# Eight array places for the state matmuls of a chunked scan, with pairs of PSUM banks and other opening fillers

## The chip, the core and the metric

The kernel runs on one core of a Trainium2 chip. A core has a matmul engine (TensorE: PE for the matmuls, PEld for the loads of their weights in the traces), a vector engine (VectorE, DVE), a scalar engine (ScalarE, ACT), a general engine (GpSimd, POOL) and a queue engine (SyncE, SP) that here issues nearly all DMAs. Each works through its own instructions in order; semaphores order them against each other. The metric is the device time of one execution in microseconds (us). Data lie in an on-chip memory of 128 partitions (SBUF); matmuls write to eight accumulation banks (PSUM) of 128 partitions by 512 float32 values each, which VectorE and ScalarE read.

## What is computed

A chunked linear-attention scan over 4 batches of 8 heads, 768 positions, head size 32 and state size 16, followed by a feed-forward network on the 3072 tokens of 256 features. The weights of the network arrive as float64 and are split on the chip into a high and a low part.

```python
for c in range(nc):                       # chunks of the sequence
    cum = np.cumsum(la, axis=-1)          # la: log of the decays of the chunk
    L = np.exp(cum[:, :, :, None] - cum[:, :, None, :]) * causal
    M = np.einsum('bhin,bhjn->bhij', Cc, Bc) * L
    y[:, :, sl] = einsum('bhij,bhjd->bhid', M, xc) + einsum('bhin,bhnd->bhid', Cc, state) * exp(cum)
    state = decay_full * state + sum_j(B_j x_j decay_from_j)
...
h = (x @ w1) * (x @ w2) @ w3              # x: the scan's y, heads side by side
return h @ w_out
```

## The kernel before

**Tiling.** The kernel uses chunks of 48 positions, so there are 16 chunks, and two of them make a slice: 8 slices of 96 positions of 4 batches, 384 tokens. Heads go in pairs: one head of a pair lies on partitions 0 to 63, the other on 64 to 127 (16 rows of carried state and 48 of x each), so that 16 pairs cover the 32 heads. w3 and w_out are first multiplied into one matrix (steps `v.M`), and then each slice needs only `up` (x by w1 and w2, 8 tiles of features, two halves, tasks `l{slice}.{tile}.0` and `.1`, six float32r matmuls of 384 columns each), a gate (`.a` a copy on ACT, `.g` a multiply on DVE, `.h` and `.l` the split into high and low parts) and `down` (tasks `z{slice}.{0..2}`, with `y...` for the way out).

**A chunk's steps** (function `chunk`, from L371). `D0`, `D1`: the differences of the cumulative logs by matmul, 384 columns into one bank each. `E0`, `E1`: their exponential on ACT into R. `B0`, `B1`: POOL scales B's columns in R. `C`: the products of B and C, 16 float32 matmuls on 32-row by 64-column places of the array (eight places), into four banks. `M0` to `M3` (`weigh`, L400): DVE multiplies R by one of these banks each, 128 by 192. `Y` (L424): py, 32 float32 matmuls, each with one head's 64 rows as weights' rows, 32 columns and 64 moving columns, so on a 64-row by 32-column place. Its output is the next state (16 columns) and y transposed (48 columns). The column quarter q of four goes with row half q % 2, so four of the eight such places are used, and all output goes to one bank. `Z` (L437): DVE transposes the state part of py; `x0` to `x3` (`carry`, L440): four copies of it into XE for the next chunk, on the engine that the plan names. `h`, `l` (L449, L450): ACT and DVE split y out of py into the high and low parts that `up` takes.

**Banks.** `at_of` (L222) gives the bank of step k of chunk c (0, 1: D; 2 to 5: C; 6: py). From chunk 7 on these are banks 0 to 3 and, for py, bank 7; before, they rotate through banks 0 to 3. Banks 4 to 6 are a ring of three on which `up` and `down` tiles take turns in the order of the text `ORDER` (L22, L187 to L196). Bank 7 holds the product of w3 and w_out until that is done.

**Order.** The order of all engines is written out by hand: `PLAN` (L29) names every task, and each engine runs its part in the order of the text. A suffix names the engine (`:a` ACT, `:v` DVE, `:p` POOL). `+12` stands for 12 matmuls of bfloat16 zeros, 512 columns wide (`keep_clock`, L635): they compute nothing that is used.

**Weights.** `from_f64` (L458) makes the tasks of a piece of 128 by 512 float64 weights: `.D` its DMAs on SP into one of six staging slots (ST), `.A` and `.Y` mostly on ACT, `.L`, `.S` on DVE, `.H` the high part on the engine that the plan names and `.P` the low part on DVE. w0 to w7 are the pieces of w1 and w2, o0 to o3 those of w_out, v0 to v15 those of w3. `a.save` writes the cumulative logs to DRAM, and the tasks `c{n}.K`, from chunk 2 on, load them back chunk by chunk; `c{n}.X` loads x, `c{n}.T` B and C, `s{n}.N` B again in another layout. All are issued by SP in the order of the plan.

Of the kernel before, what the change touches and what calls it, by code (L numbers as in the profile page):

```python
# [7 lines left out]
F32 = mybir.dt.float32  # L8
# [6 lines left out]
ALU = mybir.AluOpType  # L15
# [19 lines left out]
w3.A:a l0.1.0 c1.Z w3.Y:a w2.L s1.N c1.x0:p c3.X w2.S c1.x1:p c2.D0 l0.1.1 c1.x2:p c2.E0 l0.0.g w2.H:p l0.1.a  # L35
w5.D w4.A:a w3.L c2.D1 c1.x3:p w2.P:v c2.E1 w4.Y:a +2 l0.2.1 w3.S w3.H:v c2.C c3.T w3.P:v c2.B1 w6.D c2.B0
l0.2.0 c2.M3 w7.D c2.M2 c2.M0 c2.M1 c3.D1 l0.2.a o1.D w4.L c3.D0 c3.E1 c2.Y w4.S c3.E0 c3.B1 l0.1.g c3.B0 o0.D
l0.3.1 w5.A:a c2.Z w4.H:p o2.D l0.2.g c2.h c2.x0:p l0.3.0 w4.P:v w5.Y:a c2.x3:p c4.T c2.x1:p c2.l c2.x2:p l0.4.0
l0.3.a w5.L w5.S c3.C l0.4.a c4.K l0.3.g w6.A:a w5.H:p l0.4.1 c3.M0 c3.M1 w6.Y:a c3.M3 c3.M2 l0.4.g c3.Y o3.D
w5.P:v w6.L l0.5.0 c3.Z w6.S c3.x0:p c3.h s2.N l0.5.1 c3.x2:p l0.5.a c3.l w6.H:p o1.A:a w7.A:v l1.0.1 c3.x3:p  # L40
o1.Y:a w6.P:v c3.x1:p v0.D l1.0.0 l0.5.g w7.Y:a o1.L o1.S l1.1.0 l1.0.a w7.L o0.A:a v3.D l1.1.1 w7.S o0.Y:a
l1.0.g w7.H:p o2.A:v v1.D l0.6.0 l1.1.a w7.P:v o2.Y:a c5.T l1.1.g l0.6.1 c4.X o0.L l0.6.a o0.S c5.K o1.H:a
# [58 lines left out]
def kernel(  # L101
# [88 lines left out]
    for op in ORDER.split():  # L190
        sl, ft = map(int, op.split(".")) if "." in op else (int(op), None)
        for k in [(sl, tk) for tk in range(NTT)] if ft is None else [(sl, ft, i) for i in range(2)]:
            pl_bank[k] = bank[4 + ring % 3]
            ring += 1
# [521 lines left out]
```

## Time and profile before

| | us |
|---|---|
| time, median of 3 runs | 281.46 (281.34 to 282.18) |
| the profiled execution's own time | 281.39 |
| its span, first to last instruction | 279.6 |

The page of the profile gives the busy time of each engine, the last chain of work and the costliest groups of instructions. In a group's row, `out<-in` are the program's tiles, then the form, the count, the busy time in us, the mean of one in ns, and the idle time of the engine before them with who ended it. Two things help in reading it: a float32 matmul leaves two records where a float32r one leaves one, and the end of a matmul is modelled and includes its way through the array, so that matmuls overlap; what one costs is read from the start of one to the start of the next. Three groups that belong to the steps of the change:

```profile
L158 PEld LDWEIGHTS bank<-rr,xe 64*32 64x32 f32 x1024 | 15.2, 107 | 5.5 <-issue 3.9
L394 ACT ACTIVATE rr<-bank 128x384 f32<-128x384 f32 x32 | 14.9, 492 | 9.8 <-PE bank L158 8.3
L167 POOL TENSOR_TENSOR rr<-bn,rr 128x128 f32<-128x128 f32 x32 | 15.9, 507 | 47.2 <-ACT rr L394 46.3
```

They are the weight loads of Y, the exponentials E and the scalings B.

### The profile page before, as it was taken

What the parts mean: (1) busy time and instruction counts of PE and PEld (TensorE: products, weight loads), DVE (VectorE), ACT (ScalarE), POOL (GpSimd) and SP (SyncE); (2) the same over time, 40 slices, a digit from 0 to 9 for tenths busy, and PEclk for the clock granted to TensorE, in tenths of its full rate; (3) what the DMA queues carried; (4) which work ended last, traced back from release to release, by engine and by line L of the source; (5) the groups of instructions that cost most, each with busy time, mean ns of one, the idle gap of its engine ahead of it and who ended that gap; (6) DMA issues with size and microseconds to landing.
All of it is one profiled execution on the core that took longest, in us unless ns stands there. A gap on an engine that the chain in (4) does not pass through costs nothing.

```text
span 279.6 us, 7296 instructions
## 1 busy us (share of the span) xinstructions
PE 273.8 (98%) x2957; PEld 242.6 (87%) x2957; DVE 155.5 (56%) x326; ACT 145.8 (52%) x280; POOL 105.6 (38%) x160
## 2 busy tenths in 40 slices
PE   8999999999999999999999999999999999999995
PEld 2466899998999998889998999999998998999884
DVE  5699999999999858354544153415251442122110
ACT  5496799999547377243561354335441543134211
POOL 8806550424423269581241236204520533044200
PEclk9999999999999999999999999999999999999999
DMA  5968988788831010225130320222011000100011
GB/s 164 289 189 255 351 281 267 221 293 283 267 115 39 4 52 0 70 77 160 33 80 21 78 69 16 89 71 82 11 30 45 15 2 0 43 15 0 21 49 46
DMA packets 22710, 29.31 MB, mean 105 GB/s; under 512 B 5524, under 2 KB 12948, under 8 KB 22676
## 3 DMA queue, kind: packets, MB, share of 16 engines
q1 hardware_dynamic: 22628, 28.81, 33.8%
q8 instruction: 23, 0.38, 0.6%
q14 instruction: 11, 0.09, 0.1%
q10 hardware_dynamic: 48, 0.03, 0.0%
HBM read 25.54 MB, written 3.29 MB: 103 GB/s over the span
## 4 chain that ended last, share of the span: by engine, by line
PE 90%; DMA 3%; SPq 2%; DVE 2%; issue 1%; POOL 0%; ACT 0%; DVEq 0%
PE bank L158 90%; SPq L161 2%; DMA cd<-gf 2%; DMA st<-in_w_dram 1%; DVE vl L167 1%; DVE gf L167 0%; DVE rr L167 0%; DVE wo L167 0%; POOL gf L167 0%; ACT rr L394 0%; POOL rr L167 0%; ACT ob L164 0%; DVE zz L437 0%; POOL gf L164 0%; DVE zero L268 0%
## 5 line engine op out<-in xcount | busy, mean ns | idle before, releaser
L158 PE MATMUL bank<-xt,w 128*128 128x384 f32 x768 | 146.2, 341 | 0.5
L158 PEld LDWEIGHTS bank<-xt,w 128*128 128x128 f32 x768 | 132.1, 188 | 5.9 <-DVE w L167 0.9
L167 POOL TENSOR_TENSOR g<-gf,g 128x384 fp32r<-128x384 f32 x52 | 55.6, 1081 | 62.1 <-ACT g L164 59.1
L158 PE MATMUL bank<-wo,g 128*128 128x256 f32 (+1 forms) x392 | 68.5, 334 | 0.0
L158 PEld LDWEIGHTS bank<-wo,g 128*128 128x128 f32 x392 | 59.5, 188 | 7.9
L167 DVE TENSOR_TENSOR gf<-gf,bank 128x384 f32<-128x384 f32 x64 | 35.2, 550 | 50.2 <-PE bank L158 45.0
L164 ACT CAST g<-gf 128x384 fp32r<-128x384 f32 x64 | 31.2, 514 | 36.5 <-DVE gf L167 36.4
L164 ACT COPY gf<-bank 128x384 f32<-128x384 f32 x64 | 31.5, 494 | 16.3 <-PE bank L158 16.2
L167 DVE TENSOR_TENSOR ob<-ob,bank 128x256 f32<-128x256 f32 x23 | 9.6, 419 | 45.4 <-ACT ob L164 45.4
L164 ACT COPY ob<-bank 128x256 f32<-128x256 f32 x24 | 9.0, 373 | 49.0 <-PE bank L158 46.6
L167 POOL TENSOR_TENSOR rr<-bn,rr 128x128 f32<-128x128 f32 x32 | 15.9, 507 | 47.2 <-ACT rr L394 46.3
L164 ACT COPY st<-st 128x512 uint16<-128x512 uint16 x23 | 31.6, 1398 | 1.1 <-DVE mag L482 0.7
L167 DVE TENSOR_TENSOR rr<-bank,rr 128x192 f32<-128x192 f32 x64 | 19.2, 348 | 5.6 <-POOL rr L167 2.7
L164 POOL COPY xe<-zz 16x256 f32<-16x256 f32 x28 | 14.6, 520 | 16.9 <-DVE zz L437 15.9
L497 DVE SCALAR_TENSOR_TENSOR mag<-mag,st 128x512 uint32<-128x512 uint32 x28 | 20.2, 723 | 0.7
L158 PEld LDWEIGHTS bank<-rr,xe 64*32 64x32 f32 x1024 | 15.2, 107 | 5.5 <-issue 3.9
L394 ACT ACTIVATE rr<-bank 128x384 f32<-128x384 f32 x32 | 14.9, 492 | 9.8 <-PE bank L158 8.3
L158 PE MATMUL bank<-wfh,vh 128*128 128x256 f32 x64 | 18.8, 293 | 0.0
L158 PE MATMUL bank<-rr,xe 64*32 64x64 f32 x1024 | 18.2, 218 | 0.4 <-issue 0.4
L158 PE MATMUL bank<-wfh,vl 128*128 128x256 f32 x64 | 17.9, 279 | 0.0
L158 PE MATMUL bank<-wfl,vh 128*128 128x256 f32 x64 | 17.9, 279 | 0.0
L479 ACT ACTIVATE mag<-st 128x512 f32<-128x512 f32 x22 | 15.3, 704 | 0.4 <-DMA st<-in_w_dram 0.3
(68 smaller groups left out, 210.4 us busy)
## 6 DMA issues: line engine op xcount, KB each, us to landing
st<-in_w3t_dram SPq DMA_DIRECT2D x16, 512.0 KB
st<-in_w_dram SPq DMA_DIRECT2D x16, 256.0 KB
xe<-in_x_dram SPq DMA_DIRECT2D x32, 96.0 KB
bc<-in_Bt_dram SPq DMA_DIRECT2D x8, 320.0 KB
bc<-in_Ct_dram SPq DMA_DIRECT2D x8, 320.0 KB
bn<-in_Bn_dram SPq DMA_DIRECT2D x8, 256.0 KB
st<-in_w_out_dram SPq DMA_DIRECT2D x4, 512.0 KB
out_dram<-ob SPq DMA_DIRECT2D x16, 96.0 KB
```

Of the source, the lines that this page charges most:

```text
L158: return tc.keep_in_program_order(nc.tensor.matmul(*args, **kw))
L161: return ins({None: nc.sync, "a": nc.scalar}[eng].dma_start(*args))
L164: return ins(nc.scalar.copy(*args) if eng == "a" else {"v": nc.vector, "p": nc.gpsimd}[eng].tensor_copy(*args))
L167: return ins({"v": nc.vector, "p": nc.gpsimd}[eng].tensor_tensor(*args))
L394: ins(nc.scalar.activation(R[:, hf * G8:(hf + 1) * G8, N:], v["pd", hf], AF.Exp))
L479: ins(nc.scalar.activation(v["mag"], v["wh"], AF.Copy, scale=2.0 ** -112))
L497: ins(nc.vector.scalar_tensor_tensor(mi, mi, 3, v["wh"].bitcast(U32), ALU.logical_shift_left, ALU.bitwise_or))
```

## The change

**Y on eight places.** The host swaps the two heads of each pair in odd batches, so that their rows lie in the other half. Y then goes through pairs of batches: for the even batch the column quarters 0, 1, 2, 3 with row halves 0, 1, 0, 1, and for the odd one the quarters 1, 0, 3, 2 with row halves 0, 1, 0, 1, eight places in a row. Even batches go to one bank and odd ones to another. Before chunk 7 these are banks 0 and 1; from chunk 7 on, bank 7 and one bank of the ring, for which `ORDER` has an entry (`c7` to `c15`). Each carry becomes two copies (on two engines where the plan names two). Before chunk 7, `Z`, `h` and `l` stay one instruction each, over the pair of banks; from chunk 7 on each becomes two, one for each bank, the ring's bank first.

**C and M in pairs of banks.** Banks 0 and 1, and 2 and 3, become one tile each of two banks. C always goes to these four; `M0` and `M1` multiply two banks at once. D of chunks 2 to 15 always uses banks 2 and 3.

**Order.** In slice 3 the plan takes the order of the later slices, with Y of one chunk directly ahead of C of the next. In slices 4 to 6, `Z`, `h` and `l` of a chunk come right behind Y and ahead of the next chunk's M.

**Opening.** The first fillers are 2 bfloat16 zero matmuls and 2 of float32 zeros (`*2`) in place of 12; `+7` before Y of chunk 1 becomes `*1 +3` and `+4` before the first `up` becomes `*1`. The float32 zeros lie in the last staging slot and are set by one more memset at the start. The fillers write bank 6 in place of 7. The DMAs of w2 (`w2.D`) are issued behind `a.save` in place of before it. The H step of w0 goes to POOL, `w1.Y` behind `c1.h`, and `k.R1` behind the carries of chunk 0.

The diff, cut to its core:

```diff
-+12 c0.C b.m01:v b.m10:v c0.D0 c1.X b.m11:v k.L1 w2.D c0.D1 a.scan c0.E0 k.R0 a.t0:p c1.D0 a.r0:p c0.E1 c0.B0
-w0.A:a c0.B1 c1.D1 c0.M0 c0.M1 a.t1:p c1.E0 c0.M2 a.r1:p c0.M3 w0.Y:v c1.E1 c0.Y c1.B0 a.save c1.B1 w0.L k.R1
-c1.C c2.X c0.Z c0.x0:v c0.x1:a w3.D c0.x3:a c0.x2:v c1.M0 c0.h c1.M1 w1.A:a c1.M2 c1.M3 w0.S w1.Y:a +7 c1.Y
-w0.H:v w0.P:v c1.h c2.K w2.A:a c0.l c1.l +4 l0.0.0 w2.Y:a w4.D w1.L w1.S l0.0.1 c2.T l0.0.a w1.H:v w1.P:v c3.K
++2 *2 c0.C b.m01:v b.m10:v c0.D0 c1.X b.m11:v k.L1 c0.D1 a.scan c0.E0 k.R0 a.t0:p c1.D0 a.r0:p c0.E1 c0.B0
+w0.A:a c0.B1 c1.D1 c0.M0 a.t1:p c1.E0 a.r1:p c0.M1 w0.Y:v c1.E1 c0.Y c1.B0 a.save c1.B1 w2.D w0.L c1.C c2.X c0.Z
+c0.x0:va c0.x1:ap c0.x2:vp c0.x3:ap k.R1 w3.D c0.h c1.M0 w1.A:a c1.M1 w0.S *1 +3 c1.Y w0.H:p c1.h w1.Y:a c2.K
+w2.A:a c0.l w0.P:v c1.l *1 l0.0.0 w2.Y:a w4.D w1.L w1.S l0.0.1 c2.T l0.0.a w1.H:v w1.P:v c3.K w3.A:a l0.1.0 c1.Z
...
-l4.0.h c11.B1 l4.1.1:4 l4.1.a l4.0.l:p l4.2.0:4 l4.1.g l4.1.h l4.2.1:4 l4.2.a l4.1.l:p c10.Y l4.2.g l4.2.h c11.C
-c10.Z s6.N l4.2.l:p l4.3.0:4 c10.h c11.M0 c11.M1 c10.x0:a c10.x1:v c10.x2:a l4.3.1:4 c10.x3:v l4.3.a c13.K c10.l
+l4.2.0:4 l4.1.g l4.1.h l4.2.1:4 l4.2.a l4.1.l:p c10.Y l4.2.g l4.2.h c10.Z c10.h c10.l c11.C s6.N l4.2.l:p
+l4.3.0:4 c11.M0 c10.x0:a c10.x1:v c10.x2:a l4.3.1:4 c10.x3:v l4.3.a c13.K l4.4.0:4 c11.M1 l4.3.g l4.3.h l4.4.1:4
...
+    PAIR = [ps.tile([P, 2, 512], F32, name=f"bank{i}") for i in range(2)]
+    bank = [PAIR[i // 2][:, i % 2] for i in range(4)] + [ps.tile([P, 512], F32, name=f"bank{i}") for i in range(4, 8)]
...
+    zerof = ST[:, NST - 1, 0:512]
...
         if c < CPS:
-            return bank[(0, 1, 2, 3, 4, 5, 6 if c == 0 else 1)[k]]
-        return bank[(7 * c + k) % 4 if c < CPS * (NLAG + 1) - 1 else (0, 1, 0, 1, 2, 3, 7)[k]]
+            return bank[((4, 5, 5, 7), (6, 4, 0, 1))[c][k]]
+        if k == 3 and c >= CPS * (NLAG + 1) - 1:
+            return pl_bank[False, (c,)]
+        return bank[(2, 3, 0 if c < CPS * (NLAG + 1) - 1 else 7, 1)[k]]
...
+        def weigh(hf):
+            t = R[:, hf * G8:(hf + 1) * G8, N:].rearrange("p (k g) s -> p k g s", k=2)
+            pc = PAIR[hf][:, :, :G8 // 2 * T].rearrange("p k (g s) -> p k g s", s=T)
+            tt("v", t, pc, t, ALU.mult)
...
+                for b2 in range(B2):
+                    for u, qs in enumerate(((0, 1, 2, 3), (1, 0, 3, 2))):
+                        po = py[0][:, u] if len(py) == 1 else py[1 - u][:, 0]
+                        for q in qs:
+                            h2 = (q + u) % 2
+                            g, rows = (2 * b2 + u) * HP + 2 * kt + q // 2, slice(64 * h2, 64 * h2 + 64)
+                            mm(po[32 * q:32 * q + 32, kt * B2 + b2], xe[rows, g], R[rows, g, :], start=True, stop=True)
...
+                for t, u in zip(py, us):
+                    ins(nc.vector.transpose(ZZ[:, u].rearrange("p u k b d -> p u (k b) d"), t[:, :, :, 0:32]))
...
+                for u, eu in zip((1, 0), e * 2):
+                    h2 = (q + u) % 2
+                    copy(eu, xn[64 * h2:64 * h2 + N, u, q // 2], ZZ[32 * q:32 * q + N, u].rearrange("p k b d -> p b k d"))
...
-    def keep_clock(n):
+    def keep_clock(n, z):
         for _ in range(n):
-            mm(bank[7], zero[:, 0:P], zero, start=True, stop=True)
+            mm(bank[6], z[:, 0:P], z, start=True, stop=True)
```

More of the change, by code (lines that the diff above doesn't have):

```diff
@@ L190 @@
     for op in ORDER.split():
-        sl, ft = map(int, op.split(".")) if "." in op else (int(op), None)
-        for k in [(sl, tk) for tk in range(NTT)] if ft is None else [(sl, ft, i) for i in range(2)]:
-            pl_bank[k] = bank[4 + ring % 3]
+        kind, k = op[0], tuple(map(int, op.strip("cz").split(".")))
+        for k in [k + (i,) for i in range(2)] if kind not in "cz" and len(k) == 2 else [k]:
+            pl_bank[kind == "z", k] = bank[4 + ring % 3]
             ring += 1
-        if ft is None:
-            DOWNS.append(sl)
+        if kind == "z" and k[0] not in DOWNS:
+            DOWNS.append(k[0])
     passing = ctx.enter_context(ExitStack())
```

166 lines of the change are left out of this document (87 added, 79 removed), and 3 rows, old and new, of the table ORDER.

## The prediction

> **What bounds the kernel now.** I read the page first: the busy times, the chain that ended last, the row of the small matmuls that the change touches.
>
> ```profile
> span 279.6 us, 7296 instructions
> PE 273.8 (98%) x2957; PEld 242.6 (87%) x2957; DVE 155.5 (56%) x326; ACT 145.8 (52%) x280; POOL 105.6 (38%) x160
> PE 90%; DMA 3%; SPq 2%; DVE 2%; issue 1%; POOL 0%; ACT 0%; DVEq 0%
> L158 PE MATMUL bank<-rr,xe 64*32 64x64 f32 x1024 | 18.2, 218 | 0.4 <-issue 0.4
> ```
>
> TensorE is busy 98% of the span, and 90% of the last chain is its own work. The fourth line is py, step Y: 1024 records for 16 chunks, 64 a chunk; each of its 32 float32 matmuls leaves two. An average over stages hides who else is full, so next the table by stage (length, then busy us of PE, PEld, DVE, ACT, POOL, each with its count; the second row counts only instructions that write or read the carried states), and the chain of waits in order of time near its end.
>
> ```profile
> 28.00:77.00 49.00, 48.82 (x570) 45.00 (x559) 47.82 (x94) 42.69 (x61) 19.10 (x33) 1.00 0.87 281
> 27.00:77.00 50.00, 4.68 (x256) 3.87 (x256) 0.00 (x0) 0.00 (x0) 8.91 (x16) 1.00 0.87 281
> 76.53 0.47 DVE gf L167
> ...
> 77.05 199.22 PE bank L158 x2034
> ```
>
> There are three stages. From 28 to 77 us, while the float64 weights are converted, **two** engines are full: DVE works 47.82 of 49.00 us, and the chain reaches PE at 77.05 by way of a DVE instruction. From 77.05 to the end PE works 199.22 us without a break, while DVE has 155.5 - 47.8 = 107.7 us of work for the other 230. Before 28 us lies an opening of fillers and waits. Y of four chunks, 2 to 5, falls between 27 and 77 us (x256), two lie before and ten behind. So a PE saving counts in full after 77 us, and before only as far as DVE can follow.
>
> **The main part: py on eight places.** PE's timeline in two late slices (start, length, group):
>
> ```profile
> 155.80 2.25 PE L158 MATMUL bank<-xt,w 128*128 128x384 f32 x12
> 157.89 0.50 PE L158 MATMUL bank<-rd,ld 102*128 102x384 bf16 x2
> ...
> 187.35 4.49 PE L158 MATMUL bank<-xt,w 128*128 128x384 f32 x24
> 191.77 1.10 PE L158 MATMUL bank<-rr,xe 64*32 64x64 f32 x64
> 192.79 0.59 PE L158 MATMUL bank<-bc 32*64 32x96 f32 x32
> 193.31 4.43 PE L158 MATMUL bank<-xt,w 128*128 128x384 f32 x24
> 197.58 0.50 PE L158 MATMUL bank<-rd,ld 102*128 102x384 bf16 x2
> ```
>
> From its start to the next start Y takes 192.79 - 191.77 = 1.02 us and C 0.52. Inside them, by short windows (PE busy with the matmuls that run in the window, old ones that still drain included; the first three rows count only Y, the last two only C):
>
> ```profile
> 191.76:191.84 0.08, 0.07 (x4) 0.07 (x8) 0.00 (x0) 0.00 (x0) 0.00 (x0) 1.00 0.00 0
> 191.84:191.90 0.06, 0.06 (x8) 0.06 (x12) 0.00 (x0) 0.00 (x0) 0.00 (x0) 1.00 0.00 0
> 191.90:191.96 0.06, 0.06 (x12) 0.06 (x11) 0.00 (x0) 0.00 (x0) 0.00 (x0) 1.00 0.00 0
> ...
> 192.79:192.92 0.13, 0.13 (x8) 0.13 (x16) 1.00 0.00 0
> 192.92:193.17 0.25, 0.25 (x32) 0.25 (x31) 1.00 0.00 0
> ```
>
> Y runs in rounds of four: the second and third window are cut at a round's length, 0.056 us, and each adds four to the four of the first. 16 rounds: 0.08 for the first, 14 x 0.056, 0.16 for the last until C starts, together 1.02. C, with its eight places, starts eight in its first 0.13 us and the other 24 in 0.25 (x32 with the first eight still draining): rounds of eight every 0.083 for 96 columns, 0.87 ns a column, the pace of Y (0.056 / 64 = 0.87). So eight places at once cost no more than four, in four banks and with a weight load before each matmul. Eight starts must fit into one round: four took under 0.03 (x4 in a 0.06 window), C's eight under 0.083; I take them to fit 0.056.
>
> Y after: eight rounds. First 0.08 to 0.13 (Y's own and C's), six times 0.056, the last 0.16 to 0.22 (192.79 + 0.52 less its last round's start at 192.79 + 0.13 + 2 x 0.083). That is 0.58 to 0.69; I take 0.64, **0.38 saved a chunk**, 6.1 over 16. Bounds: 0.44 at best; below, a loss (the slower rival).
>
> **Merged blocks.** In slice 3, C of 9, Y of 8, Y of 9 and C of 10 stood apart between up matmuls; now Y of 8 and C of 9, and Y of 9 and C of 10, are neighbours. Twelve up matmuls alone take 157.89 - 155.80 = 2.09, so 24 would take 4.18; behind C they took 197.58 - 193.31 = 4.27, and between rd and Y 191.77 - 187.35 = 4.42. A switch of the array's tiling thus costs 0.09 to 0.33 in and out; about 0.2 for each merged pair, **0.4** (0.2 to 0.6).
>
> **DVE, ACT, POOL.** The four M become two, and each carry two halves. Z, h and l stay one instruction each up to chunk 6, over a pair of banks, and become two from chunk 7 on.
>
> ```profile
> L167 DVE TENSOR_TENSOR gf<-gf,bank 128x384 f32<-128x384 f32 x64 | 35.2, 550 | 50.2 <-PE bank L158 45.0
> L167 DVE TENSOR_TENSOR ob<-ob,bank 128x256 f32<-128x256 f32 x23 | 9.6, 419 | 45.4 <-ACT ob L164 45.4
> L167 DVE TENSOR_TENSOR rr<-bank,rr 128x192 f32<-128x192 f32 x64 | 19.2, 348 | 5.6 <-POOL rr L167 2.7
> L437 DVE STREAM_TRANSPOSE zz<-bank 128x256 f32<-128x256 f32 x15 | 6.7, 446 | 4.2 <-PE bank L158 4.2
> L164 ACT COPY gf<-bank 128x384 f32<-128x384 f32 x64 | 31.5, 494 | 16.3 <-PE bank L158 16.2
> L164 ACT COPY ob<-bank 128x256 f32<-128x256 f32 x24 | 9.0, 373 | 49.0 <-PE bank L158 46.6
> L164 POOL COPY xe<-zz 16x256 f32<-16x256 f32 x28 | 14.6, 520 | 16.9 <-DVE zz L437 15.9
> ```
>
> DVE: (550 - 419) / 128 = 1.02 ns an element, so 0.16 us is fixed. M costs 2 x 0.55 = 1.10 for 4 x 0.35 = 1.39, 0.29 less; but the rr row is busy only 19.2 for 64, 0.30 each where they overlap, and then it is 0.10 less, or nothing if two long ones overlap no further. I take **0.15 less a chunk**, bounds 0 and 0.3. From chunk 7 on l costs 2 x 0.35 - 0.55 = 0.15 more and Z 0.16 more; that and ACT's part ((494 - 373) / 128 = 0.95 ns an element, 0.13 fixed, so h +0.13 and each carry half about the same) lies where both engines wait for PE. In 28 to 77 us the carries are POOL's; a half costs at most a second full 0.52, 2.1 a chunk, 8 us beside the 30 that POOL is idle in these 49. So all but M is hidden; without that cover it would be 0.3 a chunk on DVE.
>
> From chunk 7 on, one half of py takes a bank of the ring of three on which up and down turn. Its next user is the third up group after Y: 0.52 for C and two groups of 6 x 0.174 = 1.04 each, 2.6 us. That half is read first: after the DVE multiply that may be running (0.55), transpose 0.3, h 0.31, l 0.35, and the other half's transpose between, 1.8 in all. Cover 0.8 us: cost nothing.
>
> **The opening.**
>
> ```profile
> 1.30 5.30 PE L158 MATMUL bank<-zero 128*128 128x512 bf16 x12 [1.30 <-DVE zero L268]
> 6.53 0.59 PE L158 MATMUL bank<-bc 32*64 32x96 f32 x32
> 7.31 0.91 PE L158 MATMUL bank<-gf,ls 112*128 112x384 f32 x2
> 8.16 0.33 PE L158 MATMUL bank<-im,ld 48*128 48x384 bf16 x1
> ...
> 13.03 1.68 PE L158 MATMUL bank<-zero 128*128 128x512 bf16 x7
> 8.11 0.97 SPq L161 DMA_DIRECT2D st<-in_w_dram  x2
> 9.69 1.31 DVE L167 TENSOR_TENSOR rr<-bank,rr 128x192 f32<-128x192 f32 x4 [1.48 <-POOL rr L167]
> 11.30 4.94 DMA cd<-gf
> 16.85 0.70 ACT L479 ACTIVATE mag<-st 128x512 f32<-128x512 f32 x1
> ```
>
> Twelve bfloat16 zeros fill 1.30 to 6.53, 0.44 each; later seven take 1.68, 0.24 each. A float32 matmul of 384 columns, two records, takes 8.16 - 7.31 = 0.85, so one of 512 about 1.13, and 2.1 to 2.3 at the early pace. Now two and two: 0.9 + 4.2 to 4.6, less the weight loads hidden in a row of them: PE is free between 5.8 and 6.8, not 6.53. What that moves is limited: the first M starts at 9.69 because of POOL, which nothing speeds. The later fillers (1.13 + 3 x 0.24 for 7 x 0.24, and 1.13 for four) are 0.2 longer each, in waits for DVE and ACT.
>
> w2's two DMAs leave SP at 8.11 now; moved behind the save of the cumulative sums they leave at 11.7, and then only c2's x and w3 queue behind them. The save, 4.94 us to its landing, no longer stands behind w2's 512 KB, and the loads that wait for it come earlier; if w2 too needs 4.94, it lands at 16.6, just ahead of ACT's turn at 16.85. Cover 0.2 us; without it ACT and what is queued behind are late by the rest. The smaller moves stay inside the same bounds: the zeros of the float32 fillers lie in the staging slot of w5, whose DMA waits for the last such filler, many issues ahead of its need; the fillers write bank 6 in place of 7, so those before l0.2.1 wait for an ACT copy out of it, but that up group goes to the same bank and waits anyway, and only the 2 x 0.24 is late; w0's H leaves DVE for POOL; w1's Y goes behind chunk 1's h on ACT, which frees h and delays what ACT does for w1 and w2. In slice 3 the loads of later chunks leave SP in another order, slices ahead of their use. I take **0.3 saved** in the opening (between 0.9 and -0.6).
>
> **The sum**, against the profiled execution's own 281.39 (span 279.6, 1.8 around it), 0.1 off the median 281.46. Opening -0.3. Chunks 2 to 5, before 77 us: PE would give 4 x 0.38 = 1.5, but DVE follows only by the shorter M of four chunks, 0.6, and by what of its 1.2 idle closes up, say 0.4: -1.0. Chunks 6 to 15: 10 x 0.38 = 3.8; merges 0.4. Together -5.5: **275.9**, itself 274.9 to 277.2.
>
> **Rivals.**
> - *DVE follows* (PE's saving counts everywhere, the opening's two Y too): 16 x 0.38 + 0.4 + 0.3 = 6.8, 274.6. For it: PE's own waits in that stage can't be told from DVE's order by these rows. Against: 47.82 of 49.
> - *The clock stays low.* The early zeros ran at half the pace of the later ones, so full pace comes with several us of work. If the new fillers end before B and C land and PE idles, the four D blocks that follow, 0.85 and more each by the gf row, run up to twice as long: 4 x 0.85 = 3.4 at most, 2.5 if pace comes back within them: 278.4. The Trainium skill ("TensorE: Matmul & The Clock Gate", Part 1) says that the clock doubles only after a busy window of about 3.4 us whose phase is free; the half pace until about 6.5 agrees.
> - *A new wait on the ring*: if the readers of py need over 2.6 us, 0.4 in each of nine chunks is 3.6: 279.5.
> - *The change doesn't do what it says*: the two halves of one column group don't overlap and Y stays at 1.02: 281.4 less 0.3, 0.4 and DVE's 0.1 to 0.3 is 280.5.
> - *Slower*: with every place working, the next weights can't be loaded behind, and each round costs what C's first did, 0.13: 7 x 0.13 + 0.22 = 1.13, +0.11 x 16 = 1.8, with merges at -0.4 and M hidden 282.8. It decides once a round of eight exceeds 0.112. Against: C's later rounds at 0.083. The Trainium skill ("TensorE: Matmul & The Clock Gate", Part 3, The mechanism) lets a weight load overlap running matmuls only when the row group differs; with both halves always working that rule gives this rival. By that rule the rounds of Y would be longer already, since it uses both row halves now; the windows show its loads hidden, so the trace disagrees.
>
> **How the numbers follow.** Forecast 0.53, DVE follows 0.19, clock 0.08, ring 0.05, no overlap 0.08, slower 0.07. The range 273.8 to 279.5 holds the first four, 0.85; its low end is the second at Y's bound of 0.44 a chunk. A measurement here tells about 0.3%, 0.84 us: under 280.6 is faster. The first four and, on its edge, part of the no-overlap case are faster, 0.88; the rest of that case 0.05; slower 0.07.
>
> **What would show it.** Y's start to the next start 0.58 to 0.69 late in the run, 1.02 if there is no overlap; the profile page's py row near 18.2 - 6 = 12 us. The up matmul that now starts at 77.05 comes about 1.3 earlier if DVE binds, 1.8 or more if it follows. PE waits after 77 us still none. DVE over 48 us of the 28 to 77 stage, or an idle PE ahead of 6.5 us, would prove me wrong.

## The result and the profile after

The changed kernel was timed on two occasions. The first time its six runs gave a median of 278.51 us (278.08 to 280.12) beside 281.51 for the kernel before, a ratio of 0.990 (95% interval 0.988 to 0.993). The second time ten runs gave 280.16 us (278.26 to 282.21) beside 281.47, 0.995 (0.992 to 0.998). So the change makes the kernel **faster by 1.3 to 3.0 us**, about half or less of the 5.5 that were forecast, and its runs lie further apart: the middle half of its ten spans 279.5 to 280.9, that of the 15 runs of the kernel before beside them 281.3 to 281.6. Both halves of this, the missing gain and the spread, need a cause.

The profiled execution took 279.71 us (span 278.0), one of the longer runs. Its page:

```profile
span 278.0 us, 7341 instructions
PE 269.6 (97%) x2943; PEld 239.1 (86%) x2947; DVE 154.2 (55%) x324; ACT 149.1 (54%) x305; POOL 115.8 (42%) x195
...
q8 instruction: 23, 0.38, 0.6%
...
PE 74%; DVE 11%; DMA 7%; issue 3%; POOL 2%; SPq 1%; ACT 1%; DVEq 0%; POOLq 0%; ACTq 0%
...
L163 POOL COPY xe<-zz 16x128 f32<-16x128 f32 x59 | 22.7, 384 | 14.9 <-DVE zz L457 12.5
...
L166 DVE TENSOR_TENSOR rr<-bank,rr 128x384 f32<-128x384 f32 x32 | 17.2, 551 | 4.3 <-POOL rr L166 2.4
...
L157 PE MATMUL bank<-rr,xe 64*32 64x64 f32 x1024 | 14.6, 224 | 1.0 <-issue 0.9
```

The row of py fell from 18.2 to 14.6 us, not to 12. M costs 2 x 0.54 a chunk (17.2 / 32) for 4 x 0.30. POOL's carries rose from 14.6 us in 28 copies to 22.7 in 59. PE's own work is 74% of the last chain, where it was 90%: DVE and DMA have come into it. The table by stage (same columns as before) and the chain of waits around the point where DVE hands over to PE:

```profile
28.00:77.00 49.00, 47.48 (x553) 43.82 (x555) 45.87 (x86) 42.91 (x62) 22.34 (x44) 1.00 0.84 274
```

```profile
77.69 0.47 DVE gf L166
78.16 0.04 issue
78.21 196.42 PE bank L157 x1923
```

From the handover on PE works 196.42 us without a break instead of 199.22: **2.8 us gained**, with no wait of PE. But the handover comes at 78.21 instead of 77.05, **1.16 us later** in this execution, and DVE, which was to be full, works 45.87 of the 49 us in place of 47.82. 1.16 lost and 2.80 gained are the 1.6 us between the two spans. Late in the run, PE's timeline:

```profile
162.20 0.86 PE L157 MATMUL bank<-rr,xe 64*32 64x64 f32 x64
162.99 0.59 PE L157 MATMUL bank<-bc 32*64 32x96 f32 x32
163.51 0.79 PE L157 MATMUL bank<-xt,w 128*128 128x384 f32 x3
```

Y takes 0.79 us from its start to the next start, C 0.52 as before: 0.23 saved a chunk where 0.38 was forecast. Ten chunks of 0.23 and 0.4 to 0.5 for the merged blocks are the 2.8.

Between 30 and 40 us two things stand out, one on PE's timeline and one on DVE's:

```profile
33.22 1.13 PE L157 MATMUL bank<-rr,xe 64*32 64x64 f32 x63 [0.16 <-POOL xe L163]
35.20 0.24 PE L157 MATMUL bank<-rr,xe 64*32 64x64 f32 x1 [0.86 <-issue]
35.38 1.85 PE L157 MATMUL bank<-xt,w 128*128 128x384 f32 x9
```

```profile
38.56 0.69 DVE L166 TENSOR_TENSOR w<-mag,w 128x512 fp32r<-128x512 f32 x1 [1.19 <-POOL w L163]
```

PE stops ahead of the very last matmul of c3.Y, waiting for nothing that the profile shows ("issue"); two records start 1.08 us apart there, where 0.06 is the most that is usual. And DVE's w6.P waits 1.19 us for POOL's w6.H, where it waited 0.50 in the kernel before:

```profile
37.33 0.69 DVE L167 TENSOR_TENSOR w<-mag,w 128x512 fp32r<-128x512 f32 x1 [0.50 <-POOL w L164]
```

The opening gives the third place to look at. PE's timeline of the changed kernel, and the rows of the kernel before with its first up matmul and its c2.Y:

```profile
15.88 4.42 PE L157 MATMUL bank<-xt,w 128*128 128x384 f32 x18
20.75 0.34 PE L157 MATMUL bank<-rd,ld 102*128 102x384 bf16 x1 [0.46 <-DMA ld<-cd]
20.79 1.36 PE L157 MATMUL bank<-xt,w 128*128 128x384 f32 x6
23.03 0.32 PE L157 MATMUL bank<-rd,ld 102*128 102x384 bf16 x1 [0.88 <-ACT rr L401]
...
27.09 0.86 PE L157 MATMUL bank<-rr,xe 64*32 64x64 f32 x64
```

```profile
17.03 3.96 PE L158 MATMUL bank<-xt,w 128*128 128x384 f32 x18
...
27.07 1.10 PE L158 MATMUL bank<-rr,xe 64*32 64x64 f32 x64
```

The first up matmul comes 1.15 us earlier, but by c2.Y (27.09, before 27.07) nothing of that is left. Between the two, DVE waits for ACT, and ACT for a piece of weights:

```profile
20.58 0.67 ACT L510 ACTIVATE mag<-st 128x512 f32<-128x512 f32 x1 [1.11 <-DMA st<-in_w_dram]
22.69 0.43 DVE L523 TENSOR_SCALAR st<-st 128x512 int32<-128x512 int32 x1 [1.56 <-ACT st L163]
```

### The profile page after: what moved, and what is told of

It is laid out like the page before. It is cut to its first block, busy times and chain, and to the rows that moved or that the text cites. A ratio compares the mean times of both kernels' runs of the same rounds, so it can differ in the third digit from the quotient of the medians.

```text
span 278.0 us, 7341 instructions
## 1 busy us (share of the span) xinstructions
PE 269.6 (97%) x2943; PEld 239.1 (86%) x2947; DVE 154.2 (55%) x324; ACT 149.1 (54%) x305; POOL 115.8 (42%) x195
## 4 chain that ended last, share of the span: by engine, by line
PE 74%; DVE 11%; DMA 7%; issue 3%; POOL 2%; SPq 1%; ACT 1%; DVEq 0%; POOLq 0%; ACTq 0%
PE bank L157 74%; DMA st<-in_w_out_dram 3%; DVE mag L528 3%; DVE st L523 2%; DMA st<-in_w_dram 2%; DVE gf L166 2%; DVE vl L166 2%; DMA bc<-in_Bt_dram 1%; POOL xe L163 1%; DMA bn<-in_Bn_dram 1%; SPq L160 1%; DVE wfl L166 1%; DVE rr L166 1%; ACT st L163 0%; DVE w L166 0%
## 5 line engine op out<-in xcount | busy, mean ns | idle before, releaser
L166 POOL TENSOR_TENSOR g<-gf,g 128x384 fp32r<-128x384 f32 x55 | 58.5, 1073 | 59.9 <-ACT g L163 57.9
L163 POOL COPY xe<-zz 16x128 f32<-16x128 f32 x59 | 22.7, 384 | 14.9 <-DVE zz L457 12.5
L166 DVE TENSOR_TENSOR rr<-bank,rr 128x384 f32<-128x384 f32 x32 | 17.2, 551 | 4.3 <-POOL rr L166 2.4
L157 PEld LDWEIGHTS bank<-rr,xe 64*32 64x32 f32 x1024 | 11.6, 105 | 5.9 <-issue 3.7
L157 PE MATMUL bank<-rr,xe 64*32 64x64 f32 x1024 | 14.6, 224 | 1.0 <-issue 0.9
```

Of the source, the lines that this page charges most:

```text
L157: return tc.keep_in_program_order(nc.tensor.matmul(*args, **kw))
L163: return ins(nc.scalar.copy(*args) if eng == "a" else {"v": nc.vector, "p": nc.gpsimd}[eng].tensor_copy(*args))
L166: return ins({"v": nc.vector, "p": nc.gpsimd}[eng].tensor_tensor(*args))
```

## The experiments

There were twelve runs, one of them the changed kernel once more. A time is compared with the kernel before on the same chip, whose median was 281.42 to 281.57 each time. `y_twice` (288.23 us) adds work; `y_bf16` (280.24), `less_data` (278.37) and `carry_whole` leave some out and return something else. The first three were timed once. Positions inside a kernel are read from one profile each.

### What limits Y: 64 more pairs, and the same in bfloat16

The starts inside one Y of the changed kernel (162.20) show where 0.79 comes from: ns from its first matmul, some of the 64.

```
record     1   2  ...   8    9  ...  16   17  ...  25  ...  32   33   34   35   36  ...  60   64
start      0   7       47   80      127  136      192      239  268  324  332  349      576  643
```

Four rounds of eight run, the first in 0.080 and the others in 0.056, as forecast; then something breaks: a gap, and behind it at best two records every 16.6 ns, and only one every 16.6 ns at both ends of this half.

In both kernels the last six chunks change. `y_twice`:

```diff
-            for kt in range(KT):
+            for kt in [i % KT for i in range(KT * (2 if c >= 10 else 1))]:
```

> In the last six chunks each Y sends its 32 matmuls twice, the second time over the same results. Theory 'supply': PE holds some 16 pairs of weight load and matmul ready while the long matmuls before run, and after these a pair comes only every 16.6 ns (the pace in the second half of Y in the changed kernel), whatever it does. Then the second copy goes at 16.6 ns from its first matmul on: Y takes 0.79 + 32 x 0.0166 = 1.32 us, and no round of it is at 56 ns. Rival 'rounds': the second half of Y (the other head pairs, the other columns) is slow by itself. Then the second copy begins with four quick steps of 56 ns again, as the first does, and Y takes 0.79 + 0.645 = 1.44 us.

`y_bf16` has the same loop and

```diff
+                            l, r = (zero[rows, 0:32], zero[rows, 0:64]) if c >= 10 else (xe[rows, g], R[rows, g, :])
```

> In the last six chunks Y is replaced by 64 bf16 matmuls of zeros with the same shapes, places and banks (so y and the state of these chunks are left out); each leaves one record instead of two. Theory 'supply': after the first 16 or so a pair comes every 16.6 ns as in fp32, about 48 x 0.0166 + 0.25 = 1.05 us for the block. Rival 'array': what takes 16.6 ns a pair is the two passes of fp32 in the array; one pass is at least twice as quick, 64 pairs at no more than 8.3 ns, 0.53 us or less and the switch of 0.14 behind it, about 0.65 us.

PE's timeline, first of `y_twice`, then of `y_bf16`:

```profile
161.31 1.48 PE L157 MATMUL bank<-rr,xe 64*32 64x64 f32 x128
162.73 0.59 PE L157 MATMUL bank<-bc 32*64 32x96 f32 x32
```

```profile
163.88 0.68 PE L157 MATMUL bank<-zero 64*32 64x64 bf16 x64
164.50 0.59 PE L157 MATMUL bank<-bc 32*64 32x96 f32 x32
```

By the lengths, 1.42 and 0.62 us, both runs went to the rivals (1.44 and 0.65). The starts say otherwise:

```
y_twice    1 to 32: 0 to 239 ns, rounds of 80 and 56   33 to 64: 267 to 609   65 to 128: 626 to 1266, no round of 56 among them
y_bf16     1 to 32: 0 to 122 ns, rounds of 38 and 29    33: 226                33 to 64: 226 to 484, one every 8.3 ns
```

In `y_bf16` identical matmuls run at some 3.8 ns each up to the 32nd, stop for 104 ns, and then come every 8.3 ns to the end. So the array can do them more than twice as fast as they arrive, and it is not the second half of the operands: `y_twice` has no quick rounds when its first half comes round again. What holds is **supply**: 32 pairs of weight load and matmul are ready when a Y behind long matmuls starts, and behind these a pair comes every 8.3 ns. The loads speak for late instructions and against a limit in the array's output: in the slow half of `y_bf16` loads and matmuls take turns at 230, 234, 238, 242, 246 and 251 ns, one instruction every 4.2 ns, though a load puts out nothing. The expected numbers were wrong because a float32 matmul was taken for one pair. It is two: the 2943 + 2947 records make 5890 instructions, and 23 loads of instructions (the q8 row of the page), 16,384 bytes each, are 5890 / 23 = 256 records a load. `y_twice` issues 768 records more and has 26 loads, so 256 again. With 8.3 ns a pair, `y_bf16` becomes 0.12 + 0.10 + 32 x 0.0083 + 0.13 for the switch = 0.62, as measured. `y_twice` gains 64 x 0.0083 = 0.53 of its 0.63 so; the other 0.10 are stretches of some five records 16.6 ns apart around each turn of its loop over kt, and why they come stays unexplained.

For Y itself the starts give 0.24 for 32 pairs, 0.08 for the gap, 0.32 for the other 32 (0.27 at 8.3 ns a pair, and the same slow stretches) and 0.15 for the switch to C. The kernel before never met the limit: its rounds of four took 56 ns, 14 a pair.

### The order of Y undone

`y_fours` sends all matmuls of even batches, then all of odd ones:

```diff
-            for kt in range(KT):
-                for b2 in range(B2):
-                    for u, qs in enumerate(((0, 1, 2, 3), (1, 0, 3, 2))):
+            for u, qs in enumerate(((0, 1, 2, 3), (1, 0, 3, 2))):
+                for kt in range(KT):
+                    for b2 in range(B2):
```

> The changed kernel with one loop order of Y undone: all 16 matmuls of the even batches first, then the 16 of the odd ones, so that four array places work at a time as before, with everything else as in the changed kernel. If the gain of Y is the overlap of eight places, each Y goes back from 0.79 to 1.02 us start to next start, and the time rises by 10 x 0.23 = 2.3 us behind 78 us, to 280.6 to 281.2 us. If the gain behind 78 us came from elsewhere (the pairs of Y and C that were merged), Y's time rises but the total by less than 1.2 us.

279.89 us (279.51 to 280.24), ratio 0.995 (0.993 to 0.996). The first half of Y ran in rounds of four at 56 ns, but the odd batches' matmuls sit on the other places and began beside the last rounds of the even ones, so Y took 0.92, not 1.02. From the handover (77.05) to the end of the span its profile has 201.03 us, the changed kernel 199.8 and the kernel before 202.6. Of the 2.8 us, 1.2 therefore hang on the loop order: behind the handover the direction holds, and the size was expected too large. The total time does not show it, since the changed kernel itself took 280.16 on the same chip; its profile there lost more than that ahead of the handover, as the next sections show.

### The opening and w2

`old_opening` goes back to the old order up to the first up matmul; `w2_early` moves one task. The first diff is cut to the fillers and w2:

```diff
-+2 *2 c0.C ... c0.D1 ... a.save c1.B1 w2.D ... *1 +3 c1.Y ... *1 l0.0.0
++12 c0.C ... w2.D c0.D1 ... a.save c1.B1 ... +7 c1.Y ... +4 l0.0.0
```

```diff
-... k.L1 c0.D1 ... a.save c1.B1 w2.D w0.L ...
+... k.L1 w2.D c0.D1 ... a.save c1.B1 w0.L ...
```

> The changed kernel with the opening of before: its 12, 7 and 4 bf16 fillers, no zerof, w2's load issued ahead of c0.D1, the carries of chunk 0 and the gap work as before; Y, C, M and everything behind the opening as in the changed kernel. Theory 'given back': the new opening wins 1.15 us up to the first up matmul and loses it by the third piece's late issue, so nothing is left at c2.Y: this kernel is within 0.4 us of the changed one (278.1 to 278.9), its first up matmul starts near 17.0 us, w2 and w3 land near 17 and 18.2 us and c2.Y starts near 27.1 us. Rival 'opening pays': it is slower than the changed kernel by 0.5 to 1.2 us (279.0 to 279.7). Rival 'opening costs' (what the late weights do to the DVE-bound stretch up to 77 us): it is faster by 0.5 or more (278.0 or less).

> The changed kernel with one step moved: w2's two transfers are issued ahead of c0.D1 again, as before, and not behind a.save. Theory 'late piece': SP's 2.1 us issue of w2's second half behind cd held up c2.X, w3 and c2.K and made w2, w3 and bn late; issued early, w2 lands before 16 us and w3 near 18 us, c2.Y starts 0.5 to 1.1 us earlier than in the changed kernel (26.0 to 26.6 us), and the time is 0.3 to 1.1 us less (277.4 to 278.2). Rival 'bandwidth': the queues are full from 12 us on and the order only exchanges what is late; bc, cd or x land later by as much, c2.Y stays within 0.3 us of 27.1 us and the time within 0.3 us.

279.21 us (278.91 to 279.77), 0.991 (0.988 to 0.994), and 279.19 us (278.05 to 281.09), 0.991 (0.988 to 0.995): both lie between the two medians of the changed kernel, 278.51 and 280.16, so by time neither can be told from it. In their profiles c2.Y starts at 27.54 and 27.57. In the eight profiles that share the new opening it starts at 26.55 to 27.59, six of them at or below 26.90. Against the one profile of the old opening, with the same halved carries, the new one is thus worth 0.6 to 1.0 us there, more than the 0.3 forecast; `given back` falls, and 279.21 lies where `opening pays` expected it. The other two of the eight, 27.09 and 27.59, are the changed kernel's own two profiles, and in both **the weights come late and cost time**: ACT waits 0.29 and 0.79 us for w2 and 1.11 and 0.93 for the piece behind it, and DVE then waits 1.56 and 1.70 for what ACT makes of it (the second wait ends at 23.20, ACT's step at 23.17, though the profile puts it down to a transfer). In the six others ACT waits 0.27 at most. Issuing w2 early doesn't help either: c1.C waited 0.81 us for C of chunk 1 instead. So the theory `late piece` falls for `w2_early`, and the order exchanges what is late, as its rival `bandwidth` says, though c2.Y is 0.5 off and not within 0.3. Why the weights landed late in those two executions alone stays open.

### The stop in c3.Y

The load of PE's instructions of which 23 are on the page lies in the trace like any transfer. In each profile the one that belongs to this place (the stop is the gap between two starts less 0.06; in three_moves the idle time that the profile gives):

```
                 load of 16,384 bytes   c3.Y starts   PE goes on at      c3.Y to c4.Y   handover
before           31.74 to 32.82         33.23         34.25 (0.21)       25.03          77.05
after            32.95 to 33.93         33.22         35.20 (1.02)       26.21          78.21
after_again      33.12 to 34.10         33.49         35.46 (1.05)       26.17          78.44
w2_early         33.19 to 34.15         33.47         35.49 (1.21)       26.25          78.45
old_opening      32.33 to 33.33         33.44         34.61 (0.46)       25.52          77.74
y_bf16           33.47 to 34.59         32.83         36.06 (2.46)       28.14          79.87
y_twice          31.66 to 32.70         32.48         34.20 (0.92)       25.92          77.22
y_fours          31.02 to 31.95         32.75         no stop            25.50          77.05
no_plus2         31.02 to 31.98         32.67         no stop            25.53          76.98
less_data        30.09 to 31.12         32.62         no stop            25.49          76.89
h_early          31.26 to 32.22         32.50         33.68 (0.37)       25.10          76.40
carry_whole      30.98 to 31.95         31.94         33.27 (0.36)       25.24          75.76
three_moves      32.63 to 33.64         32.47         35.00, behind Y    26.12          77.13
shared_carries   30.82 to 31.89         32.53         no stop            24.93          76.27
```

Wherever PE stops, it goes on 1.3 to 1.5 us after the end of this load. And the place is fixed by a count, not by a matmul: in all ten profiles with a stop PE has started 474 weight loads in all when it stops. In the changed kernel's order that is ahead of the 64th record of c3.Y; in the kernel before and in `old_opening`, whose openings issue ten pairs more, it is ahead of the 54th. Three runs test this reading further: the changed kernel once more, and `no_plus2` and `less_data`:

```diff
-c2.D1 c1.x3:p w2.P:v c2.E1 w4.Y:a +2 l0.2.1 w3.S ...
+c2.D1 c1.x3:p w2.P:v c2.E1 w4.Y:a l0.2.1 w3.S ...
```

```diff
-            for i, w in enumerate((w1, w2)):
+            for i, w in enumerate((w1, w2) if ft < 6 else (w1,)):
...
-        from_f64(f"o{j}", lambda st: [(st.rearrange("p (f k) -> p f k", f=n),
-                                       w_out[n * j * P:n * (j + 1) * P, :].rearrange("(f p) k -> p f k", p=P))],
+        from_f64(f"o{j}", lambda st: [(st.rearrange("p (f k) -> p f k", f=n)[:, 0:1],
+                                       w_out[n * j * P:(n * j + 1) * P, :].rearrange("(f p) k -> p f k", p=P))],
```

> The changed kernel itself once more, beside the three below on one chip: 278.1 to 278.9 us. Its profile tells what varies by itself: c2.Y near 26.6 to 27.1 us, a stall of PE of 0.5 to 2.5 us at the end of c3.Y near 33 to 34 us.

> The changed kernel without its two fillers ahead of l0.2.1 (four PE instructions fewer, at a place where PE waits anyway). PE's instructions come in blocks of 256 from memory, and one block ends at the last matmul but one of c3.Y, where PE stood for 1.08 us in the changed kernel. Theory 'block': the border moves behind c3.Y, the stall falls on the up matmuls behind it, where PE has slack, c3.Z no longer waits for c3.Y, and the DVE-bound stretch from c3.Y to c6.Y gets 0.5 to 1.0 us shorter: 277.5 to 278.2 us. Rival 'data': c3.Y's last matmuls wait for something of their own (a carry, a bank); the stall stays at the same matmul and the time within 0.3 us of the changed kernel.

> The changed kernel with some 1.5 MB of weights not loaded between 22 and 36 us (the second halves of w6 and w7 and half of each piece of w_out are left out; what stood in the buffers is used). PE's stall at the end of c3.Y comes from the load of its next block of instructions (16,384 bytes), which began 5.3 us after the block before was entered (27.63 to 32.95 us) in the changed kernel, while the 16 transfer engines were full. Theory 'behind the data': with less data ahead of it that load begins within 3.5 us of c2.Y's end (by 31.0 us), and c3.Y runs without a stall. Rival 'burst': the load begins when PE has used a fixed number of instructions; it begins at the same distance from c3.Y's start (within 0.5 us of it), and the stall stays at 0.5 us or more.

`after_again` gave 280.16 us, above what was expected of it, with the stop of the first profile. `no_plus2` gave 278.98 us (278.23 to 280.2), 0.992 (0.990 to 0.994), above what its theory said, and its profile has no stop; but `y_fours`, which issues as many instructions as the changed kernel, had none either, and the load began at 31.02 in both; so this run alone settles nothing. Its rival, that the last matmuls wait for something of their own, falls with the count above, and with `three_moves`, which lacks the same two fillers and met a late load. PE's timeline there:

```profile
32.47 1.09 PE L154 MATMUL bank<-rr,xe 64*32 64x64 f32 x64
35.00 2.24 PE L154 MATMUL bank<-xt,w 128*128 128x384 f32 x12 [1.44 <-issue]
```

All 64 records of c3.Y are through, and the stop sits behind them: with four instructions fewer ahead of it, it moved out of Y. In `less_data` the load began at 30.09, earliest of all, and PE didn't stop. The rival, a fixed number of instructions used, falls with the other runs as well: PE had started 739 to 938 instructions when this load began. That less data ahead of it makes it early rests on this one execution, and is in line with the rest but not more. The Trainium skill ("Runtime: NRT & Kernel Launch", Instruction fetch mechanics) says that instructions come in blocks of 16 KiB over a DMA queue of the sequencer's own and that a border's cost is mostly hidden. The block's size agrees with the 256 records a load; the cost is not hidden here, 0.2 to 2.5 us at one border, since C and Y of chunk 3 are 96 of a block's 128 pairs and take 0.52 + 0.79 = 1.3 us, and the transfer engines are full here (share 1.05 in the first row of the next fence, second number from the end). That the full engines are what delays the load is not shown: between 29 and 32 us they were as full in `y_fours` (1.02), where it came early.

A long stop costs more than itself. `y_bf16`, which up to chunk 9 is the changed kernel, by windows (the granted clock is the third number from the end):

```profile
34.00:36.00 2.00, 0.00 (x0) 0.00 (x0) 0.50 (x2) 0.00 (x0) 0.00 (x0) 1.00 1.05 370
36.00:38.00 2.00, 1.94 (x7) 1.88 (x8) 1.67 (x4) 0.48 (x1) 1.00 (x3) 0.65 0.66 219
38.00:40.00 2.00, 2.00 (x8) 2.00 (x8) 0.81 (x2) 1.72 (x3) 1.83 (x4) 0.50 0.69 222
40.00:42.00 2.00, 2.00 (x13) 2.00 (x12) 1.80 (x5) 1.92 (x2) 1.22 (x4) 0.99 0.17 65
```

After this stop, 2.30 us of it with no matmul at work, the granted clock is a half from 36.6 to 40.0 us, and PE starts 8 matmuls in 2 us instead of 13; c4.Y comes 28.14 us after c3.Y instead of 26.2. In `y_twice`, where two Y and a C in a row use up more than a block, PE stood idle for 1.84 us up to 206.0 and for 1.88 up to 228.7, going on 1.4 and 1.5 us after the end of a load again, and the clock fell to a half for 3.4 us behind the first of them only. The Trainium skill ("TensorE: Matmul & The Clock Gate", Part 1) says that the clock halves after an idle window of about 3.4 us; here 1.84 and 2.30 us of idle time were enough, and 1.88 once were not. The second timing of the changed kernel lists a mean clock of 0.993 and 0.994 for its three longest runs (281.0 to 282.21) and 1.000 for its shortest. That these are such long stops is likely, but no trace of them was taken.

### The carries on POOL

`h_early` moves the cast of w6 ahead of one carry; `carry_whole` makes each of POOL's carries one copy again:

```diff
-... c3.Z w6.S c3.x0:p c3.h s2.N l0.5.1 c3.x2:p l0.5.a c3.l w6.H:p ...
+... c3.Z w6.S c3.x0:p w6.H:p c3.h s2.N l0.5.1 c3.x2:p l0.5.a c3.l ...
```

```diff
+                if CPS <= c + 1 and e == "p":
+                    h2 = q % 2
+                    copy(e, xn[64 * h2:64 * h2 + N, :, q // 2], ZZ[32 * q:32 * q + N].rearrange("p u k b d -> p u b k d"))
+                    return
```

> The changed kernel with one step moved on POOL: the cast w6.H goes behind the first carry of chunk 3, not behind the second. Theory 'carries': each carry is two POOL copies of 16x128 now (0.28 us at least, each) in place of one of 16x256, w6.H starts 37.91 instead of 36.60 us, and DVE's w6.P waits 1.19 us for it (before: 0.50). With the move that wait falls to 0.5 us or less, DVE is bound up to 77 us, and the time falls by 0.4 to 0.8 us. Rival 'slack': DVE waits for something else later by as much (the next weights, c4.Y), and the time stays within 0.3 us.

> The changed kernel, but from chunk 1 on each carry that POOL does is one copy of 16x256 again, into the row half of the even batches only (so the state of the odd batches is left out of the later chunks). Theory 'carries': the two copies of 16x128 take longer on POOL (6 in 2.3 to 2.5 us where 3 took 1.7), and the casts w2.H and w6.H behind them make DVE wait 1.5 and 1.2 us where it waited 0.5; with whole carries both waits fall to 0.5 to 0.9 us, c2.Y starts 0.4 us or more earlier (26.6 us or less), c3.Y to c4.Y takes 0.5 us less where c3.Y isn't stopped, and the time is 277.0 to 278.0 us. Rival 'data': DVE and PE wait for the weights' transfers there, and the time stays at that of the changed kernel (278.3 to 280.2 us).

`h_early`: 278.21 us (277.57 to 280.31), 0.990 (0.987 to 0.993). `carry_whole`: 277.88 us (277.3 to 278.34), 0.987 (0.985 to 0.990), its handover at 75.76, 1.29 us ahead of the kernel before. POOL's timeline of chunk 1's carries, first in the changed kernel, then in `carry_whole`:

```profile
19.79 2.33 POOL L163 COPY xe<-zz 16x128 f32<-16x128 f32 x6 [3.96 <-DVE zz L457]
22.19 0.61 POOL L163 CAST w<-mag 128x512 fp32r<-128x512 f32 x1
```

```profile
19.80 1.69 POOL L163 COPY xe<-zz 16x256 f32<-16x256 f32 x3 [3.94 <-DVE zz L457]
21.55 0.68 POOL L163 CAST w<-mag 128x512 fp32r<-128x512 f32 x1
```

Three whole carries take 1.69 us, the same three in halves 2.33, and the cast of w2 stands behind them. DVE's waits for the two casts, in `h_early` (w6 mended, w2 not) and in `carry_whole`:

```profile
22.83 0.69 DVE L163 TENSOR_TENSOR w<-mag,w 128x512 fp32r<-128x512 f32 x1 [1.51 <-POOL w L160]
```

```profile
22.26 0.69 DVE L166 TENSOR_TENSOR w<-mag,w 128x512 fp32r<-128x512 f32 x1 [0.50 <-POOL w L163]
36.13 0.69 DVE L166 TENSOR_TENSOR w<-mag,w 128x512 fp32r<-128x512 f32 x1 [0.50 <-POOL w L163]
```

The wait for w2.H is 1.51 us in `no_plus2`, `y_fours` and `less_data` too, and 1.18 in the other two profiles with this opening but for the changed kernel's own, where the late weights came first. In `h_early` DVE doesn't wait for w6.H at all, and c3.Y to c4.Y takes 25.10 us with a stop of 0.37, against 25.49 to 25.53 in the three runs that had no stop and the late cast. In `carry_whole` both waits are 0.50, as in the kernel before, and c2.Y starts at 26.03. Against the runs without a stop and with the late cast (76.89 to 77.05) its handover is 1.1 to 1.3 us earlier, although its own profile has a stop of 0.36. **That is what the halved carries cost**, in these profiles; by the medians `carry_whole` is 0.6 to 2.3 us ahead of the changed kernel.

### Two versions that leave nothing out

> The changed kernel with three steps moved and nothing left out: w2.H behind c1.x1 on POOL (it stood behind c1.x2), w6.H behind c3.x0 (h_early), and no fillers ahead of l0.2.1 (no_plus2). Theory 'carries': DVE's wait for w2.H falls from 1.5 to 0.9 us or less, c2.Y starts at 26.3 us or earlier, and with the 0.4 to 0.5 us of h_early the time is 277.2 to 278.0 us, 0.985 of before or less. Rival 'next in line': c1's last carries and c2's POOL products come as late as before, c2.Y stays at 26.6 to 27.1 us, and the time is that of h_early (278.2 us).

> The changed kernel with two moves and nothing left out: each carry of chunk 1 puts its odd half on DVE (which waits 1.5 us for w2.H there) and only its even half on POOL, and w6.H goes behind c3.x0 as in h_early. Theory 'carries': POOL is done with chunk 1's carries some 1 us sooner, w2.H starts near 21.0 us, DVE's wait for it falls to 0.6 us or less, c2.Y starts at 26.0 to 26.4 us, and the profile reaches c3.Y 0.3 to 0.6 us before h_early (32.5 us). The time is 277.4 to 278.2 us where c3.Y isn't stopped by the load of its instructions, and up to 1.5 us more where it is. Rival 'next in line': bn's landing or ACT sets the products B of chunk 2 and M behind them, c2.Y stays at 26.5 us or later and the time at that of h_early.

`three_moves` (w2.H behind `c1.x1`, `h_early`, `no_plus2`): 279.34 us (277.72 to 280.96), 0.992 (0.989 to 0.995). The wait for w2.H fell to 0.85 us, but what follows took it over, as the rival said, and the time came out above both. DVE's timeline:

```profile
22.24 0.69 DVE L163 TENSOR_TENSOR w<-mag,w 128x512 fp32r<-128x512 f32 x1 [0.85 <-POOL w L160]
25.49 1.02 DVE L163 TENSOR_TENSOR rr<-bank,rr 128x384 f32<-128x384 f32 x2 [0.68 <-POOL rr L163]
```

M of chunk 2 now waits for POOL's product B, which came behind the delayed carries; c2.Y stayed at 26.57.

`shared_carries` gives the odd halves of chunk 1's carries to DVE and has the move of `h_early`:

```diff
-... c1.x0:p c3.X w2.S c1.x1:p c2.D0 l0.1.1 c1.x2:p c2.E0 l0.0.g w2.H:p ... c1.x3:p w2.P:v
+... w2.S c1.x0:pv c3.X c2.D0 l0.1.1 c2.E0 l0.0.g c1.x1:pv c1.x2:pv w2.H:p ... c1.x3:pv w2.P:v
```

277.98 us (277.66 to 281.27; 0.990, 0.987 to 0.993), the lowest median of a version that computes everything, though its interval doesn't set it apart from `h_early` or from the changed kernel's first timing. w2.H started at 21.05, yet w2.P only at 22.84: DVE no longer waited, it was busy with the carries that it took over (0.22 to 0.55 us each, 1.4 in all), and c2.Y stayed at 26.63. So the rival's outcome came, by way of DVE's own work and not of bn or ACT. The time is that of `h_early`, with two of nine runs above 280.

## Why the prediction was only half right

The forecast was 275.9 us, 5.5 less than before, and 3.0 and 1.3 less were measured. The first median lies inside the range of 273.8 to 279.5, but among the prices of rivals that did not happen (the clock at 278.4, the ring at 279.5), so that it does is luck; the second, 280.16, lies outside. Two terms of the sum failed (Y's 0.38, and the carries that were put at nothing), the cover for w2 failed in some executions, and one cause was not in it at all.

- **Y on eight places: overlap right, size off.** The step was "Eight starts must fit into one round: four took under 0.03 (x4 in a 0.06 window), C's eight under 0.083; I take them to fit 0.056." They fit while the 32 pairs last that wait in front of PE; behind these a pair takes 8.3 ns at best, so eight take 67 or more, with a gap ahead of them. The term was 0.38 a chunk and measured 0.23, outside its 0.58 to 0.69 for Y. Over ten chunks this is **1.5 us** of the missing gain. C's rows could not warn of it: its rounds of 83 ns use a pair every 10.4 ns, slower than the supply. The rivals "no overlap" and "slower" fell: Y is neither 1.02 nor above, and the weight loads run beside full rounds.
- **Merged blocks and the ring: right.** 2.8 less 2.3 leaves 0.4 to 0.5 for the merges (0.4); it is a remainder, and no run undid the merges alone. PE never waits behind the handover, so the ring's bank was covered.
- **"So all but M is hidden" failed.** POOL's halved carries were priced well inside the bound (a half at most 0.52; measured 0.38) and then set against POOL's idle time of the whole stage. But two casts stand behind them in POOL's order and DVE behind these, and DVE was the engine that binds: **1.1 to 1.3 us**. With the carries whole, in `carry_whole`, the handover is 1.29 earlier than before, and the text had said "about 1.3 earlier if DVE binds". That the sum fits is in part luck: 1.04 of it is there by c2.Y (26.03 for 27.07), where little more than the opening's 0.3 was due, and from c2.Y to the handover it gains 0.25, with a stop of 0.36 within, where most of 1.0 was due. DVE works 47.78 of the 49 us there, 47.82 before, so the 0.4 of its idle time that was to close up did not.
- **M: near.** 1.08 a chunk for 1.20, 0.12 less (0.15).
- **The opening: undersized, and its cover thin.** The 0.3 forecast became 0.6 to 1.0 at c2.Y in six of eight profiles, of which the halved carries left 0.2 to 0.5 against the kernel before. "Cover 0.2 us" for w2 did not hold in the changed kernel's own two profiles: w2 and the piece behind it came late, and c2.Y at 27.09 and 27.59. PE did idle for 0.24 us ahead of 6.5, which the text had named as a sign against it, but for B and C to land; the D blocks behind kept their pace (1.11 us from one to the next, as before), so the clock rival fell there.
- **Not seen at all: the load of instructions.** The profile before had a trace of it, a gap of 0.27 where 0.06 is usual, at the same place in PE's count, ten records earlier in c3.Y. With Y shorter and the transfers still full, the changed kernel and its variants reach the border with the load still under way or just done: a stop of 0.4 to 1.5 us in eight of thirteen profiles, 2.5 and a halved clock in one, none in four. From stop to handover, 1.0 us of stop came out as 0.7 us in c3.Y to c4.Y.

The account: 5.5 forecast, less 1.5 (Y) and 1.15 (carries), is 2.85, or 278.6 us: the first median (278.51), and the profiles without a stop (278.56 in `no_plus2`, 278.37 in `less_data`). The stop of 1 us adds 0.7, and the late weights of the opening add 0.2 to 1.0 at c2.Y (27.09 and 27.59 for 26.55 to 26.90): 279.5 to 280.3, the changed kernel's two profiled executions (279.71 and 280.21). Which of these its other runs met was not measured, so it is an inference that the second median (280.16) comes from them, and why the second occasion was slower stays open.

## What to carry to other kernels

An engine's idle share hides nothing by itself: before a cost is called covered, look at what stands behind it in that engine's order and whether the engine that binds waits for that. Packing small matmuls onto more places of the array pays until the instructions run out; count pairs of weight load and matmul (two for a float32 one), not array time. A burst of small matmuls also uses up a block of instructions in a microsecond or two, so a gap of PE with no releaser deserves a look at the transfers of instructions.

## What the hardware showed that was not expected

- Behind long matmuls PE starts 32 pairs in 122 ns (bfloat16) or 239 ns (float32), pauses for about 0.1 us, and goes on at 8.3 ns a pair in bfloat16, and at 8.3 at best, 10 on average, in float32.
- PE stood still for 0.2 to 2.5 us at the border of a block of 256 instructions, the same place in PE's count each time, and went on 1.3 to 1.5 us after the end of that block's load, in all ten profiles with a stop there.
- 2.30 us (`y_bf16`) and 1.84 us (`y_twice`) without a matmul were enough for the clock to fall to a half, for 3.4 us; 1.88 us, once, were not.
- A copy of 16x128 on POOL takes 0.28 us at best and 0.38 on average where one of 16x256 took 0.39 and 0.52: halving the work saved a quarter.
